# A sparse attention and gated MLP kernel: three moves in the order list of the middle cycles

## The chip, the cores and the metric

The kernel runs on one core of one Trainium2 chip. The metric is the device time of one execution in microseconds. "The profile" is one execution recorded by the hardware profiler; its rows count time from the first instruction (the span).

## The reference

```
# q, k, v: (8, 8, 576, 64) = batch, heads, tokens S, head size
scores = q @ k.T / 8
heads 0-3: token i sees tokens i-31 .. i              # local
heads 4-7: token i sees i, i-32, i-64, ...            # strided
x = softmax(scores) @ v                               # to (8, 576, 512)
h = gelu_tanh(x @ w_in);  u, v = halves of h          # 512 columns each
v_n = (v - mean(v)) / sqrt(var(v) + 1e-6) * g_ln
gated = u * (w_sg @ v_n + b_sg)                       # w_sg mixes the tokens
out = x + gated @ w_out
```

## The kernel before

Everything of one batch entry b lies in SBUF; the work goes through the eight entries one after the other, and the attention of entry b+1 is woven into the MLP of entry b. What is done in what order is written out by hand in three lists of words: START (b = 0), CYCLE (run for b = 1 to 6) and LAST (b = 7). `emit` walks through a list and calls one function per word; every engine (PE/TensorE, DVE/VectorE, ACT/ScalarE, POOL/GpSimd) and every DMA queue keeps its instructions in that order. An engine waits only for semaphores of what its next instruction reads or overwrites. A word is a step and its part: lower case works on entry b, upper case on b+1, and a + means b+2. A ^ changes which of two sets of PSUM banks a step takes, and sends GpSimd's part to VectorE and the reverse where a step can run on either; with it loads go out on ScalarE's DMA queue and stores on SP's, without it the other way. The lists are not run in parallel with each other; the overlap comes from the engines running apart.

The precision of the MLP comes from splitting each float32 operand into a high and a low part, so a product is three matmuls. Names of the steps that the change and the profile rows touch:

- `g`, `ls`, `lr`, `lm`: gelu of v on ScalarE, mean and variance on VectorE, the inverse root as a chain of small operations, and the centring. `lh:i` (ScalarE) writes the high part of v_n and `ll:i` (VectorE, line 849) the low part, a subtraction of the form v·s - high with two SBUF tensors as input. Parts 0 and 1 are 256 tokens each (tile vg), part 2 the last 64 tokens (tile t).
- `u:i`: one quarter of u on TensorE (24 matmuls); `ug:i` (line 867) is its gelu on ScalarE, which frees the PSUM buffer. `s:i` (tile sg) mixes v_n over the tokens, `sm`, `sh`, `sl` gate it, `o`, `o2`, `os`, `od` are the output product, the residual, and the store. Odd b carry an extra output part (o:4), for the last 64 tokens of two entries.
- `TQ:i` (line 415): the transposes of q and k of one pair of heads on VectorE, which release the raw buffers. For the strided heads (i = 2, 3) they are written with a stride. `LQ+:i` loads q and k into raw buffers, in eight DMAs on SP; its q half takes the buffer that the q transpose ahead of it gives free, its k half that of the k transpose.
- `SS:i` (tile ss): the strided scores, 64 small matmuls per pair of heads; `SL:i` (tiles sa, sr) the local ones. `MK`, `MX`, `SB`, `EX`, `SU`, `ML` are the steps of a softmax: mask, row maximum (tile mx), subtraction, exp, sum, product. For the local heads (:0, tile sml) SB and ML run on GpSimd, EX on ScalarE, the others on VectorE. `PL`, `CL`, `VA` (tiles ptl, ol) turn the local weights and multiply them with v.
- `XD` stores x to DRAM by its pair of heads; `r` (line 910) reads 512 tokens of it back as tile xn for the residual, 1 MB, and `rt` (line 915) the last 64 as xnt. Both go out on SP and wait until the stores of all four pairs have landed; `os` reads them.

ScalarE loads a function table when it changes from gelu to exp or back; copies work under either table.

Of the kernel before, what the change touches and what calls it, by code (L numbers as in the profile page):

```python
# [51 lines left out]
"""  # L52
CYCLE = """
v1:1 PV-^:3 PW-:3 XH-:3 XL-:3 XR-:3 v1^:0 XD-^:3 xt v2:1 g:1 v2:0 ls^:1 lr:1 lm^:1 g:0 v:2 ls:0 vh vl^
lr^:0 SL:0 SL^:1 g:2 ls^:2 lm:0 lr:2 u^:1 lh:0 lm:2 MK:0 lh:1 u:0 ll:0 ll:1 ug:1 MX:0 u^:3 lh:2 ll^:2 ug:0 SB:0
TQ:2 LQ+:0 u:2 ug:3 EX:0 TQ:3 LQ+:2 SU^:0 ug:2 s^:3 rt^ ML:0 SS^:3 SS:2 TZ+:0 sm:3 s:1 MK^:3 MX:3 sh:3 SB^:3
MK^:2 EX:3 sm:1 sh:1 MX:2 SB:2 s:0 TQ+^:0 sl^:3 PL:0 LQ+:1 CL:0 SU:3 EX:2 sm:0 s:2 TZ+:1 CM^:0 sh:0 VA:1 r
sm:2 sl^:1 VA:0 sh:2 XH^:0 XH:1 LV:3 sl:0 sl:2 SU:2 XL^:1 o:0 o2^:0 XR:0 o:4 XL:0 TQ+:1
LV:2 XR:1 o:1 o2:1 ML:2 os:0 o2:4 XD^:0 os:1 os:4 o^:2 LZ+:1 od^:0 od:1 PS^:2 LZ+:0 o:3
ML^:3 XD^:1 o2:3 od^:4 CS:2 PS^:3 os^:3 PV:2 PW:2 o2:2 CS:3 LQ+:3 XH:2 os:2 XR:2 XL:2  # L60
# [41 lines left out]
def tile_sparse_attention_moe(  # L102
# [26 lines left out]
    TP = S // NCL  # L129
# [282 lines left out]
        kt = state[b, hh, "k"] = p2.tile([P, S + ST], F32, tag="kT", name=f"kT_{b}_{hh}")  # L412
        pool.memset(kt[:, 0:ST], 0.0)

    def qk_transpose(b, hh):

        for nm in ("q", "k"):
            flat = state[b, hh, "raw" + nm].rearrange("p n d -> p (n d)")
            if nm == "k" and hh < NH // 2:
                dst = state[b, hh, "k"][:, ST : ST + S]  # L420
            else:
                tt = p2.tile([P, S + ST], F32, tag=nm + "T", name=f"{nm}T_{b}_{hh}")
                state[b, hh, nm] = tt
                dst = tt[:, 0:S]
            if hh >= NH // 2:
                dst = dst.rearrange("p (c g a) -> p g a c", c=8, a=4)
            dve.transpose(dst, flat)
# [514 lines left out]
    def out_send(b, kk):  # L942
# [6 lines left out]

    STEPS = {  # L950

        "LQ": qk_load, "LP": qk_rows, "TP": qk_turn, "TC": qk_turned, "TQ": qk_transpose, "LV": v_load, "TZ": k_zeros, "LZ": v_zeros, "SL": local_scores,
        "SS": strided_scores, "MK": sm_mask, "MX": sm_max, "SB": sm_sub, "EX": sm_exp,
        "SU": sm_sum, "ML": sm_mul, "PL": local_pt, "CL": local_pt_copy, "CM": local_pt_last,
        "VA": lambda b, hh: local_pv(b, hh, range(NJ)),
# [81 lines left out]
```

## Time and profile before

| | before |
|---|---|
| median of three runs | 572.46 us (571.07 to 573.48) |
| the profiled execution, its own time | 572.76 us |
| its span, first to last instruction | 570.7 us |
| mean granted TensorE clock | 0.982 |
| TensorE / VectorE / ScalarE / GpSimd busy | 94% / 71% / 41% / 35% |

The busy shares are means over the span. A cycle of CYCLE takes 62 to 70 us; six of them make most of the time, and the first and the last list the rest. TensorE's work is in the order of the list, so a wait of TensorE inside a cycle delays all that follows it. Idle time of another engine delays the end only if TensorE comes to wait for it.

### The profile page before, as it was taken

Reading aid. Unit: us, or ns where it says so; the run is one execution under the profiler, and the core shown is the slowest. Engines: PE = TensorE matmul, PEld = TensorE weight load, DVE = VectorE, ACT = ScalarE, POOL = GpSimd, SP = SyncE. Lnnn points to the kernel's source line nnn. Section 1 sums busy time; section 2 is a strip of 40 time slices with the busy share of each in tenths; the row PEclk is TensorE's granted clock in tenths of the full one; section 3 lists DMA queues with packets and bytes.
Section 4 is the critical chain, followed back from the end, with each engine's and each line's share of the span. In section 5 each row is a group of like instructions: output and inputs, shape, how many; then the busy total and the mean of one; then the engine's idle time right before and its main releaser. Section 6 shows DMA issues by size and latency. Waiting matters only on the chain.

```text
span 570.7 us, 17039 instructions
## 1 busy us (share of the span) xinstructions
PE 537.8 (94%) x7217; PEld 484.5 (85%) x7217; DVE 407.0 (71%) x707; ACT 233.5 (41%) x361; POOL 197.9 (35%) x376
## 2 busy tenths in 40 slices
PE   5678989999899999999899999999997998999997
PEld 4567889788898899988898899988996888988995
DVE  3897899647996399937996399937994389944532
ACT  4555976323541246323541246323640245413320
POOL 5557655604340063303340063303530044302310
PEclk9967999999999999999999999999998999999999
DMA  7997576865268635666268635766374662045002
GB/s 202 242 227 169 123 166 130 194 137 124 41 98 217 122 77 94 175 129 138 40 100 214 128 72 94 179 124 138 51 155 104 127 131 71 22 108 156 1 0 92
DMA packets 253678, 70.08 MB, mean 123 GB/s; under 512 B 237793, under 2 KB 239329, under 8 KB 253602
## 3 DMA queue, kind: packets, MB, share of 16 engines
q1 hardware_dynamic: 249178, 65.00, 53.3%
q10 hardware_dynamic: 4424, 4.00, 2.2%
q8 instruction: 56, 0.92, 0.7%
q14 instruction: 20, 0.16, 0.1%
HBM read 50.09 MB, written 18.87 MB: 121 GB/s over the span
## 4 chain that ended last, share of the span: by engine, by line
PE 77%; DVE 15%; DMA 3%; issue 2%; ACT 2%; SPq 1%; POOL 0%; DVEq 0%; ACTq 0%; POOLq 0%
PE sg L83 19%; PE o L83 18%; PE v L83 15%; PE u L83 11%; PE ol L83 3%; PE os L83 3%; DVE hv L83 2%; PE pts L83 2%; DVE bnst L83 2%; PE ss L83 2%; DVE t L83 1%; DMA rowk<-in_k_dram 1%; DVE vg L83 1%; PE ptl L83 1%; PE sa L83 1%
## 5 line engine op out<-in xcount | busy, mean ns | idle before, releaser
L83 PE MATMUL sg<-wsh,vg 128*128 128x288 f32 x512 | 113.7, 297 | 0.7 <-issue 0.7
L83 PE MATMUL u<-xt,wih 128*128 128x288 f32 x512 | 103.2, 297 | 1.1 <-DVE hv L83 1.0
L83 PE MATMUL o<-woh,vg 128*128 128x512 f32 x288 | 96.0, 402 | 0.8 <-DVE ob L83 0.8
L83 PEld LDWEIGHTS sg<-wsh,vg 128*128 128x128 f32 x512 | 85.5, 188 | 1.2 <-issue 0.9
L83 PE MATMUL v<-wih,xt 128*128 128x512 f32 x256 | 84.2, 400 | 1.1 <-DVE xt L83 1.1
L83 PEld LDWEIGHTS u<-xt,wih 128*128 128x128 f32 x512 | 81.7, 188 | 2.2 <-DVE hv L83 1.1
L83 PE MATMUL u<-xt,wil 128*128 128x288 f32 x256 | 75.4, 295 | 0.0
L83 PE MATMUL sg<-wsl,vg 128*128 128x288 f32 x256 | 75.4, 294 | 0.0
L83 PEld LDWEIGHTS o<-woh,vg 128*128 128x128 f32 x288 | 54.9, 191 | 16.3 <-issue 3.5
L83 DVE TENSOR_TENSOR ob<-o,xn 128x512 f32<-128x512 f32 x32 | 21.5, 688 | 55.5 <-PE o L83 52.9
L83 PE MATMUL o<-wol,vg 128*128 128x512 f32 x144 | 57.0, 396 | 3.3 <-issue 3.3
L83 PEld LDWEIGHTS v<-wih,xt 128*128 128x128 f32 x256 | 49.2, 192 | 10.8
L83 DVE BATCH_NORM_STATS2 bnst<-hv 128x6 f32<-128x512 f32 (+1 forms) x40 | 27.0, 676 | 33.6 <-ACT hv L83 33.6
L83 PE MATMUL v<-wil,xt 128*128 128x512 f32 x128 | 50.8, 397 | 0.0
L83 PEld LDWEIGHTS sg<-wsl,vg 128*128 128x128 f32 x256 | 48.2, 188 | 0.0
L83 PEld LDWEIGHTS u<-xt,wil 128*128 128x128 f32 x256 | 48.0, 188 | 0.0
L83 ACT CAST vg<-gt 128x576 fp32r<-128x576 f32 (+2 forms) x48 | 22.9, 511 | 58.9 <-DVE gt L83 58.8
L83 ACT COPY pts<-pts 128x576 f32<-128x576 f32 x16 | 10.2, 640 | 79.4 <-PE pts L83 70.5
L83 ACT ACT_TABLE_LOAD x30 | 38.5, 1283 | 1.2 <-PEq L1019 0.7
L83 POOL MEMSET v<- 32x128 f32 x16 | 3.2, 198 | 101.1 <-PE os L83 78.6
L83 DVE TENSOR_TENSOR gt<-sg,u 128x576 f32<-128x576 f32 x32 | 23.7, 745 | 18.0 <-PE sg L83 10.3
L83 PEld LDWEIGHTS o<-wol,vg 128*128 128x128 f32 x144 | 27.4, 190 | 4.9
(141 smaller groups left out, 1068.3 us busy)
## 6 DMA issues: line engine op xcount, KB each, us to landing
v<-in_v_dram SPq DMA_DIRECT2D x62, 144.0 KB
xd<-xs SPq DMA_DIRECT2D x124, 72.0 KB
xn<-xd SPq DMA_DIRECT2D x8, 1024.0 KB
rawq<-in_q_dram SPq DMA_DIRECT2D x96, 72.0 KB
rawk<-in_k_dram SPq DMA_DIRECT2D x96, 72.0 KB
out_dram<-ob SPq DMA_DIRECT2D x21, 256.0 KB
stage<-in_moe_w_in_dram SPq DMA_DIRECT2D x8, 512.0 KB
v<-in_v_dram SPq DMA_DIRECT2D x32, 128.0 KB
```

What stands on the lines that cost most here:

```text
L83: ins = self.tc.keep_in_program_order(op(*args, **kwargs))
```

## The change

Three moves in the middle list, CYCLE; START and LAST stay as they are.

1. TQ:2 is split in TQq:2 and TQk:2. The q transpose moves up on VectorE, to stand between ll:1 and ll:2. MX:0 moves behind ll:2. VectorE's order, between the same neighbours, was ll:1, MX:0, ll:2, q, k and becomes ll:1, q, ll:2, MX:0, k; the two transposes of TQ:3 follow in both.
2. ug:2 moves ahead of EX:0 on ScalarE.
3. r and rt move up on SP: from behind LQ+:1 and from behind LQ+:2 to ahead of LQ+:0, among the first matmuls of u.

```
 CYCLE
-... MK:0 lh:1 u:0 ll:0 ll:1 ug:1 MX:0 u^:3 lh:2 ll^:2 ug:0 SB:0
-TQ:2 LQ+:0 u:2 ug:3 EX:0 TQ:3 LQ+:2 SU^:0 ug:2 s^:3 rt^ ML:0 SS^:3 SS:2 ...
-... CM^:0 sh:0 VA:1 r
+... MK:0 r rt lh:1 u:0 ll:0 ll:1 ug:1 u^:3 lh:2 TQq:2 ll^:2 MX:0 ug:0 SB:0
+TQk:2 LQ+:0 u:2 ug:3 ug:2 EX:0 TQ:3 LQ+:2 SU^:0 s^:3 ML:0 SS^:3 SS:2 ...
+... CM^:0 sh:0 VA:1

-    def qk_transpose(b, hh):
-        for nm in ("q", "k"):
+    def qk_transpose(b, hh, names="qk"):
+        for nm in names:

     STEPS = {
+        "TQq": lambda b, hh: qk_transpose(b, hh, "q"), "TQk": lambda b, hh: qk_transpose(b, hh, "k"),
```

## Rows read from the trace of the kernel before

**Rows 1.** The page: span, busy shares, one costliest group, one DMA queue.
```profile
span 570.7 us, 17039 instructions
PE 537.8 (94%) x7217; PEld 484.5 (85%) x7217; DVE 407.0 (71%) x707; ACT 233.5 (41%) x361; POOL 197.9 (35%) x376
...
L83 ACT ACT_TABLE_LOAD x30 | 38.5, 1283 | 1.2 <-PEq L1019 0.7
...
q8 instruction: 56, 0.92, 0.7%
```

**Rows 2.** Waits of TensorE over the span: total us, times, longest.
```profile
PE ss L83 <- DVE kT L83: 4.4, 3, 1.5
```

**Rows 3.** Chain of waits, 276 to 286 us (b=3): start, us, what.
```profile
276.19 2.71 DVE t L83
...
278.94 1.30 DVE qT L83
...
283.54 0.14 issue
283.67 1.36 PE ss L83 x114
```

**Rows 4.** Timeline of all engines, b=4: start, us, instruction, [idle before, releaser].
```profile
341.17 1.34 DVE L83 TENSOR_REDUCE mx<-sml 128x18 f32<-128x1152 f32 x1
341.33 1.34 ACT L83 ACTIVATE t<-hv,y 64x512 fp32r<-64x512 f32 x2 [2.52 <-POOL y L83]
342.54 0.74 DVE L83 SCALAR_TENSOR_TENSOR t<-hv,y,t 64x512 fp32r<-64x512 f32 x1
...
342.59 2.68 POOL L83 TENSOR_TENSOR sml<-sml,mx 128x1152 f32<-128x1152 f32 x1 [1.29 <-DVE mx L83]
343.32 1.38 DVE L83 STREAM_TRANSPOSE qT<-rawq 128x576 f32<-128x576 f32 x1
...
346.77 1.35 DVE L83 STREAM_TRANSPOSE kT<-rawk 128x576 f32<-128x576 f32 x1
...
348.26 0.30 PE L83 MATMUL sg<-wst,t 97*128 97x288 f32 x1
...
348.48 1.25 PEld L83 LDWEIGHTS ss<-kT,qT 64*36 64x36 f32 x128 [0.17 <-ACT u L83]
348.49 1.37 PE L83 MATMUL ss<-kT,qT 64*36 64x36 f32 x128
...
349.88 2.13 POOL L83 TENSOR_TENSOR sml<-sml,sr 128x1152 f32<-128x1152 f32 x1 [4.61 <-DVE sr L83]
...
357.33 1.15 PE L83 MATMUL ptl<-ident,sml 128*128 128x128 f32 x9
```

**Rows 5.** The same view, b=3.
```profile
274.81 1.34 DVE L83 TENSOR_REDUCE mx<-sml 128x18 f32<-128x1152 f32 x1
...
276.24 2.12 POOL L83 TENSOR_TENSOR sml<-sml,mx 128x1152 f32<-128x1152 f32 x1 [1.30 <-DVE mx L83]
...
281.91 0.30 PE L83 MATMUL sg<-wst,t 97*128 97x288 f32 x1
```

**Rows 6.** Busy us by stretch: PE, PEld, DVE, ACT, POOL, PEclk, DMA share, GB/s.
```profile
428.30:431.60 3.30, 0.03 (x1) 0.00 (x0) 3.30 (x6) 0.00 (x0) 0.82 (x1) 1.00 0.88 200
431.60:437.00 5.40, 5.37 (x17) 4.30 (x17) 0.30 (x1) 0.00 (x0) 0.00 (x0) 0.68 0.23 39
269.00:277.00 8.00, 8.00 (x62) 8.00 (x61) 7.80 (x14) 5.25 (x9) 5.63 (x15) 1.00 0.02 2
```

**Rows 7.** DMA table, 414.5 to 428.5 us: packets, MB, share of 16 engines.
```profile
DMA packets 8500, 2.27 MB, mean 162 GB/s; under 512 B 7872, under 2 KB 7872, under 8 KB 8499
...
q1 hardware_dynamic: 8499, 2.26, 73.9%
q14 instruction: 1, 0.01, 0.2%
```

**Rows 8.** Timeline of SP's DMA issues, b=5 and b=6.
```profile
423.42 0.50 SPq L83 DMA_DIRECT2D xn<-xd  x1
...
468.02 0.48 SPq L83 DMA_DIRECT2D xnt<-xd  x1
468.55 0.59 SPq L83 DMA_DIRECT2D xn<-xd  x1
```

**Rows 9.** Timeline of TensorE, first list, 102.5 to 104 us.
```profile
103.63 0.54 PE L83 MATMUL sg<-wsh,vg 128*128 128x288 f32 x2 [0.68 <-issue]
```

More of the change, by code (lines that the diff above doesn't have):

```diff
@@ L54 @@
 v1:1 PV-^:3 PW-:3 XH-:3 XL-:3 XR-:3 v1^:0 XD-^:3 xt v2:1 g:1 v2:0 ls^:1 lr:1 lm^:1 g:0 v:2 ls:0 vh vl^
-lr^:0 SL:0 SL^:1 g:2 ls^:2 lm:0 lr:2 u^:1 lh:0 lm:2 MK:0 lh:1 u:0 ll:0 ll:1 ug:1 MX:0 u^:3 lh:2 ll^:2 ug:0 SB:0
-TQ:2 LQ+:0 u:2 ug:3 EX:0 TQ:3 LQ+:2 SU^:0 ug:2 s^:3 rt^ ML:0 SS^:3 SS:2 TZ+:0 sm:3 s:1 MK^:3 MX:3 sh:3 SB^:3
-MK^:2 EX:3 sm:1 sh:1 MX:2 SB:2 s:0 TQ+^:0 sl^:3 PL:0 LQ+:1 CL:0 SU:3 EX:2 sm:0 s:2 TZ+:1 CM^:0 sh:0 VA:1 r
+lr^:0 SL:0 SL^:1 g:2 ls^:2 lm:0 lr:2 u^:1 lh:0 lm:2 MK:0 r rt lh:1 u:0 ll:0 ll:1 ug:1 u^:3 lh:2 TQq:2 ll^:2 MX:0 ug:0 SB:0
+TQk:2 LQ+:0 u:2 ug:3 ug:2 EX:0 TQ:3 LQ+:2 SU^:0 s^:3 ML:0 SS^:3 SS:2 TZ+:0 sm:3 s:1 MK^:3 MX:3 sh:3 SB^:3
+MK^:2 EX:3 sm:1 sh:1 MX:2 SB:2 s:0 TQ+^:0 sl^:3 PL:0 LQ+:1 CL:0 SU:3 EX:2 sm:0 s:2 TZ+:1 CM^:0 sh:0 VA:1
 sm:2 sl^:1 VA:0 sh:2 XH^:0 XH:1 LV:3 sl:0 sl:2 SU:2 XL^:1 o:0 o2^:0 XR:0 o:4 XL:0 TQ+:1
@@ L950, in tile_sparse_attention_moe @@
     STEPS = {
-        "LQ": qk_load, "LP": qk_rows, "TP": qk_turn, "TC": qk_turned, "TQ": qk_transpose, "LV": v_load, "TZ": k_zeros, "LZ": v_zeros, "SL": local_scores,
+        "LQ": qk_load, "LP": qk_rows, "TP": qk_turn, "TC": qk_turned, "TQ": qk_transpose,
+        "TQq": lambda b, hh: qk_transpose(b, hh, "q"), "TQk": lambda b, hh: qk_transpose(b, hh, "k"), "LV": v_load, "TZ": k_zeros, "LZ": v_zeros, "SL": local_scores,
         "SS": strided_scores, "MK": sm_mask, "MX": sm_max, "SB": sm_sub, "EX": sm_exp,
```

## The prediction

> **What bounds the kernel now.** I read the page first: TensorE is busy 94% of a 570.7 us span, no other engine more than 71% [rows 1]. So a reordering can win only what TensorE loses inside a cycle. The list of TensorE's waits names the losses that lie in the cycles: 4.4 us in three waits of the strided scores (ss, step SS) for VectorE's kT [rows 2], and one stop of 3.3 us ahead of an output matmul (o), during which no engine is waited for [rows 6]. The other waits lie in the first list, which the change doesn't touch.
>
> The chain of waits of one of the three cycles (b=3) shows how the ss wait comes about: VectorE's ll:2 (tile t) takes 2.71 us, the four strided transposes follow, and ss starts as the last one ends [rows 3]. The next cycle (b=4) runs the same VectorE instructions with t at 0.74 us, and ss starts without a wait [rows 4]. Beside t lies GpSimd's subtraction for the local scores (SB:0, tile sml), which MX:0 releases. In b=3 it starts 0.05 us after t, takes 2.12 us, and t ends only after it: 276.19+2.71 = 278.90 against 276.24+2.12 = 278.36. In b=4 it starts 0.05 us after t again, but now t is quick and the subtraction takes 2.68 us, 0.56 longer [rows 3 to 5]. So the two exclude each other, and which one loses is a matter of hundredths. VectorE lost three times in six cycles.
>
> The stop, in b=5: TensorE does nothing for 3.30 us, then runs 5.4 us at a granted clock of 0.68 (5.4 x 0.32 = 1.73 more), 5.03 us together [rows 6]. VectorE and GpSimd were working on other things and the DMA engines were 88% busy [rows 6]. In the 14 us that end with the stop's beginning, 414.5 to 428.5, the DMA table has 8,499 packets of q1 and not one of q8 [rows 7], the larger of the queues that carry instructions; over the whole run q8 has 56 packets, one per 10 us [rows 1]. I read it as TensorE out of instructions: the ol matmuls ahead of it are many and small. In that stretch SP issued the 1 MB read of x (step r), at 423.42, five microseconds ahead of the stop [rows 8].
>
> **The change, part by part,** in the clock of b=4, whose t doesn't collide.
>
> *Order on VectorE.* Before: MX:0 at 341.17, t at 342.54, then the transposes q, k, q, k, from 343.32 to 346.77+1.35 = 348.12, 4.80 us for four [rows 4]. After: the first q transpose takes MX:0's place at 341.17 and, at the 1.30 us of one that stands alone [rows 3], ends at 342.47. t takes 0.74, to 343.24; what it reads from ScalarE is the first of a pair that starts at 341.33 and takes 1.34 together, ready at 342.0 [rows 4]. MX:0 takes 1.34, to 344.6. Then k, q, k at three quarters of 4.80: 344.64+3.60 = 348.24. The work is the same, so this ends 0.1 later than in an undisturbed cycle. kT reaches ss 0.14 after its end [rows 3], at 348.38; TensorE's last sg matmul starts at 348.26 and ss at 348.49 now [rows 4]. ss starts where it does in b=4.
>
> What goes is the collision: when MX:0 now releases the subtraction, t is over, and beside it stand transposes. In b=4 the first of them ran beside GpSimd in 1.38 us, 0.08 more than alone [rows 3, 4]. The gain in a colliding cycle is the gap from the last sg matmul's start to ss, 283.67-281.91 = 1.76, less b=4's 348.49-348.26 = 0.23 [rows 3 to 5], so 1.53; three times, **4.6 us**. Bounds: 3.8, if the transposes end a quarter of a microsecond later still in every cycle (4.6 less six times 0.14), to 5.2, if ss starts 0.10 earlier in all six.
>
> The Trainium skill ("SBUF — State Buffer", section "SBUF: two separate sides") says that GpSimd and a VectorE instruction with two SBUF inputs, or in a two-port mode, take one port pair in turn, each for the whole instruction. It speaks against the change if transposes run in such a mode; by that the sum would be the slower rival below. The row of b=4 shows one beside the subtraction at nearly its own time.
>
> *ug:2 ahead of EX:0.* One gelu joins the two before it, so the gelu table need not be loaded again behind EX:0, nor the exp table ahead of EX:3: two loads of 1.283 us a cycle, 12 of the 30 [rows 1], all on ScalarE (41% busy). In b=4 the weight load of ss waits 0.17 us for this gelu (tile u, whose PSUM buffer ss takes) [rows 4]; moved up it is done before, so that ss waits for kT alone: nothing gained beyond the 0.10 in the bound. Queued behind ug:2 stands EX:0, whose input comes later anyway: MX:0's end at 344.6 and 2.12 us of subtraction make 346.8. So SU:0, and the product ML:0 behind it, come some tenths later than now. TensorE wants that product for the ptl transposes at 357.33; it ends at 349.88+2.13 = 352.01 now [rows 4]. Five microseconds of cover: nothing.
>
> *Reads of x inside u.* On SP the two reads now stand between the stores XD:3 and LQ+:0, and wait until the stores have landed; queued behind them are the q and k loads. In b=3's clock the DMA engines are 2% busy from 269 to 277 [rows 6], so the stores are in by 269, and LQ+:0 can't start before the first q transpose ends, at 274.81+1.30 = 276.1 [rows 3, 5]: 7 us for two issues of 0.5 [rows 8]. In b=6, where no q and k are left to load, the read of x already starts at 468.55 [rows 8], the same place against the cycle, and that cycle has no stop. Nothing waits; if the stores landed 5 us late it would cost only the head start of these loads.
>
> What leaves is the 1 MB from the ol stretch. The fetch that b=5's stop waited for then meets the q, k and v loads alone. The nearest row is the first list's sg behind an ol, with q and k loads in flight: TensorE stands 0.68 us for "issue" [rows 9]. I take that for b=5, and no drop of the clock: 5.03 shrinks to 0.68, **4.35 us**. Bounds: 0 (the small loads alone hold the fetch) and 5.03.
>
> The sum: 572.76, the profiled execution's own time (span 570.7 and 2.06 around it), less 4.6 and 4.35: **563.8**. The median of the runs is 572.46, 0.3 lower, which I leave as uncertainty.
>
> **Rivals.** (a) *The stop stays.* For it: the reads of x lie near ol in other cycles too, and only b=5 stops. Only the collision goes: 572.76-4.6 = 568.2. The Trainium skill ("DMA: Bandwidth & Descriptors", section "Queues, rings and completion order") has each DMA engine take turns between queues packet by packet, so that a fetch would not stand behind a whole 1 MB read; by that the sum is this rival's. The 14 us without a fetch [rows 7] speak against so light a delay, but name no culprit.
>
> (b) *The change doesn't do what it says:* t is slow by itself and moves with its 2.71 us. Then ss still waits: 568.4 with the stop cured, 572.8 without. Against: GpSimd's 2.68 in the cycle where t is quick [rows 4].
>
> (c) *Slower:* the subtraction blocks the strided k transpose as it blocked t. It then lasts as much longer as t did, 2.71-0.74 = 1.97, less the 0.11 us that kT has in hand (348.49-348.38), in all six cycles: 11.2 us of ss waits in place of 4.6, 579.4; 575.0 with the stop cured, which is +0.4%. With the stop left it decides from 1.3 us a cycle up ((4.6+2.9)/6), with the stop cured from 2.0. Against: the transpose of b=4.
>
> (d) *A new fetch stop,* where LQ+:0 now begins earlier: u uses few instructions, b=6 shows none; it would cost the 4.35 back, 568.2.
>
> **Chances.** Both gains 0.55; (a) or (d) 0.27; (b) 0.10, half with the stop cured; (c) 0.05 (its 575.0 lies at the edge and is counted as slower); 0.03 for no change by other ways. 0.5% is about what a measurement of this kernel can tell from no change, 2.9 us, so 568.2 and 568.4 count as faster: faster 0.55+0.27+0.05 = 0.87, same 0.08, slower 0.05. The range for 8 in 10 holds the first two: from 562.3 (both upper bounds: 572.76-5.2-5.03 = 562.5, and a little) to 569.0 (the lower bound alone: 572.76-3.8).
>
> **What the changed profile would show.** t at 0.75 in all cycles and the subtraction at 2.12; no ss wait for kT over 0.3; 18 table loads in place of 30; xnt and xn issued some 2 us behind XD:3's stores in every cycle; no stop of 3 us at o, and no clock below 1.00 in b=5's output. It is wrong if kT still ends ss's wait by more than 1 us, if a strided transpose takes 3 us beside the subtraction, or if an "issue" stop stands at another matmul.

## The result, and the profile after

The changed kernel takes **562.96 us** (median of four runs, 562.15 to 564.08), the kernel before 572.62 beside it (four runs, 571.07 to 573.48): ratio 0.9836, 95% interval 0.9808 to 0.9863. The forecast was 563.8 in 562.3 to 569.0. The profiled execution took 562.97 us, against 572.76. Its page, in the order of [rows 1]:

```profile
span 560.9 us, 17027 instructions
PE 535.4 (95%) x7217; PEld 482.7 (86%) x7217; DVE 401.5 (72%) x707; ACT 217.6 (39%) x349; POOL 195.7 (35%) x376
...
L83 ACT ACT_TABLE_LOAD x18 | 23.1, 1283 | 1.0 <-PEq L1020 0.7
```

VectorE has as many instructions as before and is 5.5 us less busy, GpSimd 2.2 less: what has gone is time in which one of them stood inside an instruction (three t's of 2.71 in place of 0.74 make 5.9, three subtractions of 2.68 in place of 2.12 make 1.7). ScalarE has 12 instructions fewer, all of them table loads (30 to 18).

Where TensorE's time went is read from a mark that every cycle has: the first matmul of the local scores (tile sa). The distance from one entry's mark to the next is a period; the stretch ahead of the first mark is the first list, the stretch behind the last one holds the end of b=6's work and the last list. All in us:

| | first list | b=1 | b=2 | b=3 | b=4 | b=5 | from the last mark (b=6) |
|---|---|---|---|---|---|---|---|
| before | 135.28 | 66.37 | 62.10 | 66.37 | 62.10 | 69.89 | 108.60 |
| after | 135.03 | 64.80 | 62.09 | 64.85 | 62.29 | 64.81 | 107.06 |
| gained | 0.25 | 1.57 | 0.01 | 1.52 | -0.19 | 5.08 | 1.54 |

Three stretches gain about 1.5 us: these are the three cycles whose ss waited 1.5 us [rows 2]. b=5 gains 5.1: there the stop was [rows 6]. The rest moves by a quarter of a microsecond at most. Two timeline rows of tile sa's beginning show how b=5's 64.81 is read, 453.87 - 389.07 with rounding:

```profile
389.07 1.23 PE L83 MATMUL sa<-kT,qT 64*32 64x64 f32 x96
...
453.87 1.23 PE L83 MATMUL sa<-kT,qT 64*32 64x64 f32 x96
```

The list of TensorE's waits has no row at all between 120 and 500 us (before: [rows 2] and the stop). The timeline of all engines in b=1, a cycle that lost 1.5 us before, answers to [rows 4, 5]:

```profile
140.22 0.38 SPq L83 DMA_DIRECT2D xn<-xd  x1
140.65 0.52 SPq L83 DMA_DIRECT2D xnt<-xd  x1
...
146.06 1.33 DVE L83 STREAM_TRANSPOSE qT<-rawq 128x576 f32<-128x576 f32 x1
146.23 1.34 ACT L83 ACTIVATE t<-hv,y 64x512 fp32r<-64x512 f32 x2 [2.52 <-POOL y L83]
...
147.42 0.74 DVE L83 SCALAR_TENSOR_TENSOR t<-hv,y,t 64x512 fp32r<-64x512 f32 x1
148.20 1.35 DVE L83 TENSOR_REDUCE mx<-sml 128x18 f32<-128x1152 f32 x1
149.47 1.34 DVE L83 STREAM_TRANSPOSE kT<-rawk 128x576 f32<-128x576 f32 x1
149.63 2.12 POOL L83 TENSOR_TENSOR sml<-sml,mx 128x1152 f32<-128x1152 f32 x1 [3.44 <-DVE mx L83]
149.78 0.65 ACT L83 ACTIVATE u<-u 128x576 f32<-128x576 f32 x1 [1.14 <-PE u L83]
150.45 1.28 ACT L83 ACT_TABLE_LOAD   x1
...
151.78 1.37 DVE L83 STREAM_TRANSPOSE kT<-rawk 128x576 f32<-128x576 f32 x1
151.79 1.17 ACT L83 ACTIVATE sml<-sml 128x1152 f32<-128x1152 f32 x1
...
153.16 0.30 PE L83 MATMUL sg<-wst,t 97*128 97x288 f32 x1
153.38 1.25 PEld L83 LDWEIGHTS ss<-kT,qT 64*36 64x36 f32 x128 [0.17 <-issue]
153.38 1.37 PE L83 MATMUL ss<-kT,qT 64*36 64x36 f32 x128
```

Five things are to be seen. t takes 0.74 us and ends 1.5 us before GpSimd's subtraction begins. The subtraction takes 2.12, although two transposes run beside it, and they take 1.34 and 1.35. From the first q transpose to the end of the last k transpose it is 153.15 - 146.06 = 7.09 us; the prediction's sum was 7.07. ss starts 0.22 behind the last sg. The table load lies inside the subtraction, so that the exp (151.79) follows 0.04 after what it needs (149.63 + 2.12 = 151.75). The view of tile t gives minimum, median and maximum (ns) over the eight entries; no t is slow any more:

```profile
L83 DVE SCALAR_TENSOR_TENSOR t<-hv,y,t x8: 744/745/747, 87.8 to 528.1; 64x512 fp32r<-64x512 f32 x8
```

In the place of the stop, behind the ol matmuls that start at 421.06, the windows (columns as in [rows 6]) show a TensorE that is never idle, at full clock. Two DMA tables, of 410.5 to 421.5 and of 421.5 to 423.5, show when the next packet of q8 comes:

```profile
421.00:425.00 4.00, 4.00 (x152) 3.61 (x152) 3.69 (x9) 2.38 (x6) 0.19 (x1) 1.00 0.43 101
425.00:431.00 6.00, 6.00 (x28) 4.97 (x27) 4.32 (x7) 0.00 (x0) 0.97 (x1) 1.00 0.50 101
```

```profile
q1 hardware_dynamic: 6790, 0.85, 48.2%
q14 instruction: 1, 0.01, 0.2%
```

```profile
q1 hardware_dynamic: 207, 0.05, 13.8%
q8 instruction: 1, 0.02, 3.3%
```

Here, too, 11 us go by without a packet of q8, and nothing stops. So an empty stretch like that of [rows 7] is no sign by itself. What differs is the next packet: it starts 0.9 us behind ol's beginning here (421.96), and 4.4 us behind it before the change (428.59 against 424.22), inside the stop. The DMA table of before, 428.5 to 431.6, has it:

```profile
q8 instruction: 1, 0.02, 2.8%
```

### The profile page after: what moved, and what is told of

Its sections match the earlier page's. It is cut to its first block, busy times and chain, and to the rows that moved or that the text cites. A ratio compares the mean times of both kernels' runs of the same rounds, so it can differ in the third digit from the quotient of the medians.

```text
span 560.9 us, 17027 instructions
## 1 busy us (share of the span) xinstructions
PE 535.4 (95%) x7217; PEld 482.7 (86%) x7217; DVE 401.5 (72%) x707; ACT 217.6 (39%) x349; POOL 195.7 (35%) x376
## 4 chain that ended last, share of the span: by engine, by line
PE 90%; DVE 3%; issue 2%; POOL 2%; ACT 2%; POOLq 0%; DVEq 0%; ACTq 0%
PE sg L83 21%; PE o L83 18%; PE u L83 18%; PE v L83 17%; PE ol L83 3%; PE os L83 3%; PE sa L83 2%; PE pts L83 2%; PE ss L83 2%; PE ptl L83 1%; POOL cv L83 1%; PE turnk L83 1%; DVE sml L83 1%; DVE sr L83 1%; DVE bnst L83 0%
## 5 line engine op out<-in xcount | busy, mean ns | idle before, releaser
L83 POOL TENSOR_SCALAR va<-mv 128x2 f32<-128x2 f32 (+1 forms) x16 | 10.4, 652 | 60.8 <-DVE mv L83 60.8
```

The source lines that it names most:

```text
L83: ins = self.tc.keep_in_program_order(op(*args, **kwargs))
```

## The experiments

Three parts were changed at once, so e1, e2 and e5 make one of the changes alone, e3 leaves one out, e4 leaves out a part of one, and the last three vary the suspected causes. The first four were run four to ten times against the kernel before (571.06 us, median of 16 runs, 567.19 to 574.46); their whole times are medians. The other four were run once, beside one run of before (571.82). The first list varies from run to run (133.18 to 136.56 us), so the periods, which are those of the profiled execution, say more than whole times:

| | b=1 | b=2 | b=3 | b=4 | b=5 | from b=6 | whole time | ratio to before, 95% |
|---|---|---|---|---|---|---|---|---|
| e1_order | 65.11 | 62.36 | 65.13 | 62.52 | 69.47 | 107.36 | 568.34 | 0.9935, 0.9903 to 0.9967 |
| e2_reads | 64.82 | 63.67 | 66.35 | 63.63 | 64.83 | 108.61 | 568.33 | 0.9950, 0.9913 to 0.9987 |
| e3_order_gelu | 64.81 | 62.11 | 64.82 | 62.35 | 68.90 | 107.06 | 565.29 | 0.9891, 0.9850 to 0.9933 |
| e4_no_split | 65.34 | 62.58 | 65.41 | 62.75 | 65.35 | 107.63 | 565.69 | 0.9894, 0.9860 to 0.9928 |
| e5_gelu | 66.45 | 62.11 | 64.93 | 62.11 | 68.27 | 107.06 | 568.89 | one run |
| e6_r_behind_v | 64.83 | 62.09 | 64.83 | 62.26 | 64.87 | 107.07 | 564.51 | one run |
| e7_half | 64.83 | 62.12 | 64.93 | 62.55 | 65.82 | 107.22 | 567.62 | one run |
| e8_t_behind_q | 65.34 | 62.60 | 65.30 | 62.59 | 69.15 | 107.57 | 568.79 | one run |

**e1_order: the order on VectorE alone** (the kernel before with this edit).

```diff
-... ug:1 MX:0 u^:3 lh:2 ll^:2 ug:0 SB:0
-TQ:2 LQ+:0
+... ug:1 u^:3 lh:2 TQq:2 ll^:2 MX:0 ug:0 SB:0
+TQk:2 LQ+:0
```

> VectorE's new order alone (q transpose, ll:2, MX:0, k transpose); ug:2 and the reads of x as before. My theory: t is at 0.75 us in all six cycles, but the gelu ug:2 now stands on ScalarE behind an exp whose input comes 2 us later; it ends about 1.55 us after ss could start, so ss waits for tile u in all six cycles (9.3 us) in place of three waits of 1.53 for kT. With the stop of 5 us in b=5 still there: 572.7+4.7 = 577.4. Rival, the gelu's place doesn't matter: 568.1, ss without a wait.

t is quick in all cycles, and no wait of ss is left: the theory's 577.4 was wrong, the time is the rival's. But the gelu that stayed behind the exp does cost something, at another place than expected. TensorE's waits from 130 to 480 us, and the timeline of b=1:

```profile
PE o L83 <- issue: 2.6, 1, 2.6
PE sg L83 <- ACT u L83: 1.3, 6, 0.2
```

```profile
153.67 1.37 PE L83 MATMUL ss<-kT,qT 64*36 64x36 f32 x128
...
154.51 0.65 ACT L83 ACTIVATE u<-u 128x576 f32<-128x576 f32 x1
...
155.22 0.40 PE L83 MATMUL sg<-wsh,vg 128*128 128x288 f32 x1 [0.18 <-ACT u L83]
```

The new order releases the subtraction later, so the exp comes later, and with it the gelu behind it on ScalarE: it ends at 155.16, 1.5 us after ss has started, where in b=4 of before ss's weight load began as it ended [rows 4]. ss doesn't wait for it; the sg matmul behind ss does, for tile u, in each of six cycles. The stop is still there, 2.59 us, and the granted clock behind it was 0.50 for 3.4 us.

**e2_reads: the reads of x alone** (the kernel before with this edit).

```diff
-... MK:0 lh:1 ... s^:3 rt^ ML:0 ... VA:1 r
+... MK:0 r rt lh:1 ... s^:3 ML:0 ... VA:1
```

> The reads of x alone at their new place. My theory: the stop ahead of o in b=5 and its slow clock go (5.0 us), the collisions of t with the subtraction stay, three of six or another number, as hundredths decide: 567.6, within 563 to 572. Rival, the stop hangs on the phase of the cycles and not on the reads: it stays, 572.7, and the packets of q8 keep coming late behind ol.

The stop is gone: b=5 takes 64.83, as in the changed kernel. The collisions stay, four of them here; TensorE's waits from 130 to 500 us and the view of tile t:

```profile
PE ss L83 <- DVE kT L83: 5.9, 4, 1.5
```

```profile
L83 DVE SCALAR_TENSOR_TENSOR t<-hv,y,t x8: 744/1730/2717, 89.5 to 535.0; 64x512 fp32r<-64x512 f32 x8
```

So the reads cure the stop and nothing else, and how many cycles collide is left to chance without the new order.

**e3_order_gelu: all but the reads** (the changed kernel with the reads put back).

```diff
-... MK:0 r rt lh:1 ... s^:3 ML:0 ... VA:1
+... MK:0 lh:1 ... s^:3 rt^ ML:0 ... VA:1 r
```

> The whole change except for the reads of x, which stay at their old place. My theory: no wait of ss for kT, t at 0.75 us, but the stop ahead of o in b=5 stays with 3 us and a slow clock behind it: 568.0. Rival, the stop hangs on the phase: it is gone here too, 563.0.

All periods are those of the changed kernel but b=5's, 68.90 in place of 64.81. (The median of the whole time, 565.29, lies between the two forecasts, and the five runs go from 562.66 to 569.12; the profiled one shows the stop, how deep it was in the others isn't known.) Windows of the stop and of what follows it, then the DMA tables of 410 to 423 us and of 423 to 425.7:

```profile
423.40:425.70 2.30, 0.03 (x1) 0.03 (x1) 2.30 (x5) 0.00 (x0) 0.79 (x1) 1.00 0.82 231
425.70:431.00 5.30, 5.30 (x17) 4.21 (x17) 1.26 (x2) 0.00 (x0) 0.00 (x0) 0.68 0.46 82
```

```profile
q1 hardware_dynamic: 6999, 1.78, 65.3%
```

```profile
q1 hardware_dynamic: 466, 0.68, 84.9%
q8 instruction: 1, 0.02, 2.1%
```

No packet of q8 until the stop, then one inside it, 3.9 us behind the beginning of ol: the same picture as before the change. The rival that the new order alone had shifted the cycle out of the stop falls. Against e1 the gelu's move is worth 0.25 to 0.31 us in five of the cycles and 0.17 in b=4; summed, with b=5 less its shorter stop (0.57 - 0.32), 1.6 us.

**e4_no_split: MX:0 behind ll:2, but the q transpose not ahead of it** (against the changed kernel).

```diff
-... lh:2 TQq:2 ll^:2 MX:0 ug:0 SB:0
-TQk:2 LQ+:0
+... lh:2 ll^:2 MX:0 ug:0 SB:0
+TQ:2 LQ+:0
```

> The whole change, but the q transpose of TQ:2 stays with the k transpose behind MX:0, so that VectorE's order is ll:1, ll:2, MX:0, q, k. My theory: VectorE stands about 0.8 us ahead of ll:2 for ScalarE's high part, the last transpose ends at 349.0 in b=4's clock and ss starts 0.65 us late in each of six cycles: 563.0+3.9 = 566.9. Rival, the split buys nothing because kT has slack: 563.0.

It takes 0.5 us more in each cycle, where the theory had 0.65. TensorE's waits from 130 to 500 us, and the timeline of b=2:

```profile
PE ss L83 <- DVE kT L83: 2.8, 6, 0.5
```

```profile
210.64 1.34 ACT L83 ACTIVATE t<-hv,y 64x512 fp32r<-64x512 f32 x2 [2.53 <-POOL y L83]
...
211.39 0.74 DVE L83 SCALAR_TENSOR_TENSOR t<-hv,y,t 64x512 fp32r<-64x512 f32 x1 [0.84 <-ACT t L83]
...
218.31 1.36 PE L83 MATMUL ss<-kT,qT 64*36 64x36 f32 x128 [0.44 <-DVE kT L83]
```

Moving MX:0 cures the collision by itself; the q transpose in the gap then fills the 0.84 us that VectorE would wait for ScalarE's first part of t.

**e5_gelu: ug:2 alone** (the kernel before with this edit).

```diff
-... ug:3 EX:0 TQ:3 LQ+:2 SU^:0 ug:2 s^:3
+... ug:3 ug:2 EX:0 TQ:3 LQ+:2 SU^:0 s^:3
```

> ug:2 ahead of EX:0 alone, all else as before. My theory: nothing in time, neither gain nor loss: the cycles without a collision keep 62.1 us (even b) and 64.8 (odd b), those with one 1.5 more, the stop of b=5 stays; 18 table loads. Rival, the earlier gelu lets ss start 0.1 to 0.2 earlier in cycles without a collision: periods of 61.9 and 64.6.

18 table loads, 12 fewer than before, and undisturbed cycles of 62.11 us, as before the change. Two cycles collide (ss waits 1.57 and 1.49), the stop is 1.70. So 15 us less work on ScalarE buy nothing by themselves; the gelu's place counts only with the new order on VectorE. The view of t shows the two slow ones as its maximum (2718 ns); of the six subtractions of the cycles, two take 2.12 us, those beside the slow t, and four take 2.68.

**e6_r_behind_v: the 1 MB read late** (the changed kernel with this edit): behind the first two loads of v, so that it lies in the same ol stretch as before, only later.

```diff
-... MK:0 r rt lh:1 ... LV:3 sl:0
+... MK:0 rt lh:1 ... LV:3 r sl:0
```

> The whole change, but the 1 MB read goes out behind LV:3, some 4 us later than before the change, in the middle of the output matmuls. My theory, that the read stood ahead of one fetch of instructions that falls due as ol begins: no stop in b=5, its period 64.8. Rival, 1 MB anywhere near ol holds the fetch: a stop of 2 us or more, and a slow clock.

No stop, b=5 at 64.87. TensorE's and SP's timelines:

```profile
422.52 2.30 PE L83 MATMUL ol<-ptl,v 64*64 64x32 f32 x144
```

```profile
423.87 1.42 SPq L83 DMA_DIRECT2D v<-in_v_dram  x2
425.33 0.39 SPq L83 DMA_DIRECT2D xn<-xd  x1
```

The read is issued 2.8 us after ol begins, in e3 0.6 before it (418.72 against 419.29), and moves as many bytes. The packet of q8 starts 1.0 us after ol begins, ahead of the read. What counts is not that 1 MB runs beside these matmuls, but that it was issued ahead of that packet.

**e7_half: half of the read at the old place, half at the new** (against the changed kernel; rh reads 256 tokens).

```diff
-... MK:0 r rt lh:1 ... VA:1
+... MK:0 rh:0 rt lh:1 ... VA:1 rh:1
```

> The whole change, but the second half of the read, 512 KB, goes out at its old place behind LQ+:1. My theory, the fetch waits for what stands ahead of it: half the transfer takes some 1.4 us less than 1 MB at 380 GB/s, so the stop of 2.3 to 3.3 becomes 0.9 to 1.9 us, period of b=5 65.7 to 67.5. Rival, it is not the amount: a stop of 2.3 us or more, or none.

The stop is 0.83 us and the period 65.82, 1.0 over the changed kernel. TensorE's timeline:

```profile
423.01 2.30 PE L83 MATMUL ol<-ptl,v 64*64 64x32 f32 x144
...
427.95 0.39 PE L83 MATMUL o<-wol,vg 128*128 128x512 f32 x1 [0.83 <-issue]
```

Half the bytes at the old place leave less than half of the stop (2.27 in e3), and the granted clock stays at 1.00 behind it. (The whole time of this run, 567.62, is 3.6 us over its span of 564.0, where the changed kernel has 2.1; its first list is 136.56.)

**e8_t_behind_q: t made to start in the middle of the subtraction** (the kernel before with this edit: the q transpose between MX:0 and ll:2).

```diff
-... ug:1 MX:0 u^:3 lh:2 ll^:2 ug:0 SB:0
-TQ:2 LQ+:0
+... ug:1 MX:0 u^:3 lh:2 TQq:2 ll^:2 ug:0 SB:0
+TQk:2 LQ+:0
```

> As before the change, but with the q transpose between MX:0 and ll:2, so that the subtraction on GpSimd has always begun when t's turn comes. My theory, that the two exclude each other and the first holds on to the end: t takes 1.2 to 1.5 us in all six cycles (it waits for the rest of 2.12 us and 0.5 of its own), the subtraction 2.12; ss waits for kT 0.4 to 0.6 in every cycle; never 2.7. Rival, t is slow by itself by turns: a mix of 0.75 and 2.7.

t takes 1.43 to 1.46 us in all six cycles, and all six ss wait 0.43 to 0.45. Timeline of b=2:

```profile
212.09 1.33 DVE L83 STREAM_TRANSPOSE qT<-rawq 128x576 f32<-128x576 f32 x1
212.25 2.12 POOL L83 TENSOR_TENSOR sml<-sml,mx 128x1152 f32<-128x1152 f32 x1 [1.30 <-DVE mx L83]
213.46 1.46 DVE L83 SCALAR_TENSOR_TENSOR t<-hv,y,t 64x512 fp32r<-64x512 f32 x1
...
218.67 1.36 PE L83 MATMUL ss<-kT,qT 64*36 64x36 f32 x128 [0.45 <-DVE kT L83]
```

t begins 0.91 us before the subtraction ends (214.37) and ends 0.55 after it; in b=3 of before it begins 0.05 before the subtraction and ends 0.54 after it [rows 3, 5]. The end of t hangs on the end of the subtraction, not on its own length. A t that is slow by itself (rival b) would have kept 2.7.

## Why the prediction was right

**The collisions: 4.6 us, measured 1.57 + 1.52 + 1.54 = 4.63.** The mechanism is shown from three sides: t is 0.745 us wherever MX:0 stands behind it (after, e1, e3, e4, e6, e7), 2.7 by turns where both start together (before, e2, e5), and 1.43 to 1.46 where it starts in the middle (e8); the subtraction takes 2.68 where t got ahead. That the transposes are not shut out, on which rival (c) turned, is in the timeline of b=1: 1.34 and 1.35 us beside a subtraction of 2.12. The rule of the Trainium skill ("SBUF — State Buffer", section "SBUF: two separate sides") that one of the two holds the port pair for its whole instruction agrees with each of these numbers, as long as the strided fp32 transposes are not counted among the instructions that want the pair. Which of the two gets it can't be read off the recorded starts: t's is 0.05 us ahead of the subtraction's where it wins and where it loses.

**The stop: 4.35 us, measured 5.08.** The mechanism was right, the size too small, and one of its signs was weak: the 14 us without a packet of q8 [rows 7] lie between packets 15.1 us apart (413.48 and 428.59), and in the changed kernel, which doesn't stop there, 11.9 us lie between two (410.05 and 421.96). The prediction left a stop of 0.68 us, taken from a row of the first list [rows 9]; none was left. That row was the wrong neighbour: the same place in the first list stands 1.22 us after the change, while b=5 doesn't stand at all. In the first list the packet of q8 starts 1.9 us behind ol's beginning before the change and 2.4 after it, without a 1 MB read ahead of it; in b=5 it is there at 0.9.

What the runs showed in its place is that the length of the stop goes with the start of this packet, and that the packet comes late where the read was issued ahead of it. Times of b=5 from the beginning of ol, in us; TensorE's stop, where there is one, always begins at 4.1:

| | read issued | packet of q8 starts | stop |
|---|---|---|---|
| before | -0.80 | 4.37 | 3.30 |
| e1_order | -0.87 | 4.23 | 2.59 |
| e3_order_gelu | -0.56 | 3.92 | 2.27 |
| e8_t_behind_q | -0.55 | 3.66 | 2.02 |
| e5_gelu | -0.55 | 3.21 | 1.70 |
| e7_half (512 KB) | -0.58 | 2.60 | 0.83 |
| after, e2_reads, e4_no_split | -26.77 to -25.87 | 0.90 to 0.98 | none |
| e6_r_behind_v | 2.81 | 0.98 | none |

In the six stops TensorE goes on 2.3 to 3.0 us after the packet's start. That only b=5 stops, the argument for rival (a), has its reason here: in b=1 to 4 of before the packet starts 0.4 to 1.4 us ahead of ol, 2 us or more before the first 2 KB packet of the read; in b=5 it falls due at 0.9 (the last two rows), when these packets have run since 0.4.

The Trainium skill's turn by packets ("DMA: Bandwidth & Descriptors", section "Queues, rings and completion order"), from which rival (a) had its 568.2, doesn't account for this: from the read's issue to the start of q8's packet 368 (e5) to 572 (e1) packets of 2 KB start, and 261 in e7 (v's loads have some of them), where the whole read is 512 of them and the half 256. So the fetch doesn't pass the read after a packet or two; a large part of the read goes out first. Rival (a) falls by e2 and e6, rival (d) by the empty list of waits.

**ug:2 ahead of EX:0 at nothing: right in the sum, wrong in the reading.** I took ss's 0.17 us for a wait for this gelu [rows 4]. The changed kernel has the same 0.17 with the gelu 3 us in the past, put down to "issue". And the move isn't idle: left where it was, the gelu would have been pushed back by the new order and would have cost 1.6 us (e1 against e3). The prediction costed it in the old order, where it is worth nothing (e5). The bound of 0.10 earlier per cycle wasn't reached either.

**The reads' new place at nothing: right.** They are issued at 140.22 and 140.65 and done on SP at 141.17, the first q transpose, which lets LQ+:0 go, ends at 147.39, and nothing waits.

The sum of the differences closes: 563.8 less 562.97 is 0.83, namely 0.73 of the stop, 0.03 of the collisions and 0.25 of the first list, less 0.18 by which b=2 and b=4 got longer (0.17 of it in the ol matmuls of b=4, 2.47 us in place of 2.30). None of the variants beats the changed kernel; e6, the nearest, has the same periods.

Some of the agreement is luck. The terms were priced from one execution, whose stop is the longest of the six. In the medians the reads are worth less, about 2.7 us alone (e2) and 2.3 on top of the rest (565.29 to 562.96), and the whole change about 8.1 against the 16 runs of before; the forecast had 9.0. The time of the changed kernel itself doesn't hang on that draw, as its profile shows neither collision nor stop.

## What to carry to other kernels

When one instruction has two durations from cycle to cycle, look at what starts beside it on the other engine; an order in which the two can't meet costs nothing and takes the chance out of it. A stop of TensorE that no engine releases, behind hundreds of small matmuls, is worth checking against the queue that carries instructions. Compare when its packet starts there with the same place of a cycle or run that doesn't stop; a stretch without packets says little. A bulk load issued just ahead of that packet can be moved: 25 us earlier or 3.4 us later both did it here. Cost a moved instruction in the order that it will stand in, not in the old one, since another edit may be what makes its place matter.

## What was not expected of the hardware

How far a bulk load holds up the fetch: with one read of 1 MB issued 1.4 to 1.8 us ahead of the 0.9 at which the packet of q8 comes elsewhere, the packet starts 2.3 to 3.5 us late and TensorE stops for 1.70 to 3.30 us; with half the read it stops for 0.83; with the read issued behind it, not at all. That q8 carries TensorE's instructions is inferred from its kind in the DMA table and from TensorE going on behind its packet. Why a packet of another queue waits for so much of a read is open: the traces don't tell which of the 16 DMA engines a packet ran on.

What a stop takes with it: after those of 3.30, 2.59, 2.27 and 2.02 us the granted clock was 0.50 (the 1.2 GHz level) for 3.4 us, while after 1.70 (e5) and 0.83 (e7) it stayed at the 2.4 GHz level. So of the 5.08 us of b=5 some 1.7 came back by the clock alone.

And the spread of the kernel before, 567.19 to 574.46 us in 16 runs against 562.15 to 564.08 in four of the changed one: three collisions in the profiled run of before, two in e5, four in e2, at 1.5 us each, and a stop between 1.70 and 3.30. Beside the gain in the mean, the change takes out these draws, as far as its four runs tell.
